# Attention scores by seven half-size products, with key and value forms streamed from HBM by group

## The chip, the cores and the metric

The kernel runs on one core of one Trainium2 chip. The metric is the device time of one execution in microseconds (us), the median of the runs of one session. The trace is that of one execution, taken by the hardware profiler. TensorE (PE) multiplies matrices into PSUM banks, VectorE (DVE) and ScalarE (ACT) work on PSUM and SBUF, GpSimdE (POOL) does small work, and SyncE (SP) issues nearly all DMAs. Each engine takes its instructions in order and waits on semaphores.

## The reference, cut to what matters

A conformer block over `x` of 2 x 4000 tokens of width 512, in bf16:

```
x1 = x + 0.5 * silu(ln(x) @ w_ff1_a) @ w_ff1_b
h = ln(x1); q = h @ w_q; k = h @ w_k; v = h @ w_v
p = softmax(einsum('btd,bsd->bts', q, k) * D**-0.5)
x2 = x1 + einsum('bts,bsd->btd', p, v) @ w_o
x3 = x2 + convolution module (gated, depthwise of 3 taps, batch norm, silu, w_pw2)
out = ln(x3 + 0.5 * silu(ln(x3) @ w_ff2_a) @ w_ff2_b)
```

The change concerns the scores, the product of queries and keys, in the third line.

## The kernel before

The 8000 tokens are cut into 16 chunks of 508 (the last of each sequence, chunks 7 and 15, has 444). The program goes through the first feed-forward chunk by chunk, then attention chunk by chunk, then the rest of the convolution and the second feed-forward. Its order is the order in which the Python code emits instructions, engine by engine; there is no planner. `tick` and `after(n, ...)` put work off by n steps.

Attention is a loop over query chunks `g` and, in each, over 32 key steps `kt` (L1587). One step emits, in this order: the scores of one key tile of 128 keys (`scores`, L1387: four matmuls of 128x508, accumulated over the four slices of the 512 features, into one of three PSUM banks s0, s1, s2 in turn); their exponentials by ACT (`exp_pair`, L1434); what is left of chunk g-1 (`units_late`); value products and Vector sums of chunk g (`units`); the query projection of chunk g+1 (`next_queries`, `q_group`); a hook; and the change of sequence (`keys_swap`). The hook puts the convolution of chunks g-1 and g-2 beside the attention (`pair`: two products `conv_b` and `conv_a`, then the taps L1936 and L1943, and a statistic L1946) and the layer norm of chunk g-1 (statistics L771, aggregate L776, a POOL step L778, L783, and four ACT normalisations).

Value products already use the seven-product scheme (Strassen's, in Winograd's form). A pair of key tiles by 508 queries is a 2x2 block matrix: two tiles by two halves of the queries. `pair_sums` (L1446) forms four block sums on DVE (L1463, bf16) for one or two pairs at a time and adds to the softmax denominators (L1476, f32); `pv` (L1481) multiplies a form of the values by a form of the exponentials, 254 columns wide, seven products over all 15 pairs, each in a bank of its own; `pv_join` (L1514, its adds L1527) puts them together at the end. The products of a chunk's last group and their joins are emitted in the first steps of the next chunk: steps 0 and 1, then two products in steps 2 to 6 (`late_third`), of which the last is read by a join (`pv_join` 5, L1527). In step 2 the denominators are split and sent through DMA transposes; five ticks later they are reduced (L1824) and inverted (L1827). `project` (L1837) multiplies the attention output of chunk g-1 by the folded weights, tile by tile in steps 9 to 12, each followed by a residual on DVE (L923) and a layer norm statistic (L771).

The feed-forward uses the same scheme for its first matmul (`ff_quad`, L1087): products 1 and 5 in one step, 2 and 6 two steps later, 7 and 3 three steps after that, 4 another three steps on, with two Vector additions (L1119) put off by one step.

The forms of the values (V4, V12) lie in SBUF for all 15 pairs. For sequence 0 DVE makes them in chunk 0 (`v_here`); for sequence 1 it makes them ahead in chunks 1 to 5, a pair in ten steps (`v_ahead`, its sums at L1552), stores them in HBM and loads them when the sequence changes.

Of the kernel before, what the change touches and what calls it, by code (L numbers as in the profile page):

```python
# [16 lines left out]
TPC = 4  # L17
# [9 lines left out]
PAIRS = 15  # L27
HC, HD, HF = CHUNK // 2, D // 2, FC // 2
# [231 lines left out]
class Conformer:  # L260
# [31 lines left out]
    def memory(self):  # L292
        nc = self.nc
        self.XR = Region(nc, "xt", (self.SLOTS + 1) * 4096)
# [40 lines left out]
        self.P30, self.b_P30 = self.XR.view(8192 + 10 * 1536, CHUNK), self.XR.buf("P30", 8192 + 10 * 1536, row)  # L335
# [62 lines left out]
        def both(Q, o, m):  # L398
            b = [Q.buf("VF", o + i * m * 2 * HD, m * 2 * HD) for i in range(PAIRS)]
            return b, [Q.view(o + 2 * j * m * 2 * HD, min(2, PAIRS - 2 * j) * m * HD).rearrange("p (n m d) -> p n m d", m=m, d=HD)  # L400
                       for j in range(FC // 2)]

        self.b_V4, self.V4 = both(C, oP, 1)
        self.b_V12, self.V12 = both(self.XR, 8192, 2)
        o = TCB * 4096
        self.hp = [A.view(o + 4 * j * 1024, min(2, PAIRS - 2 * j) * 2 * D).rearrange(
            "p (n k e d) -> p n k e d", k=2, e=2, d=HD) for j in range(FC // 2)]
        self.vhd = nc.dram_tensor("vhd", [PAIRS, 128, 2 * D], BF16, kind="Internal").ap()
        self.v4d = nc.dram_tensor("v4d", [PAIRS, 128, HD], BF16, kind="Internal").ap()
        self.v12d = nc.dram_tensor("v12d", [PAIRS, 128, 2 * HD], BF16, kind="Internal").ap()  # L410
        self.b_vhd = [Buf("vhd") for _ in range(PAIRS)]
        self.b_v4d, self.b_v12d = [[Buf("vfd") for _ in range(PAIRS)] for _ in range(2)]
# [974 lines left out]
    def scores(self, g, kt):  # L1387
        s, W = g % TCB % 2, width(g)
        kc, kj = divmod(kt, TPC)
        ps, b_ps = self.sbank()  # L1390
# [29 lines left out]
    def next_queries(self, g, kt, at):  # L1420

        if g + 1 < NCK and g != 1 and at <= kt < at + TPC:
            self.fetch_queries((g + 1) // TCB, (g + 1) % TCB, kt - at)
        if g == 0 and 24 <= kt < 24 + TPC:
            self.fetch_queries(0, 2, kt - 24)
        if g + 1 < NCK and kt in ((3, 4, 12, 14) if g == 1 else (14, 16, 18, 20)):
            self.q_group((g + 1) // TCB, (g + 1) % TCB, (3, 4, 12, 14).index(kt) if g == 1 else (kt - 14) // 2)

    def p_home(self, g, i):

        n = (16 * g + i) % self.NR
        return n, (16 * g + i) % self.NTS, self.Ft[(8 * g + i // 2) % 2], self.b_F[(8 * g + i // 2) % 2]
# [13 lines left out]
    def pair_sums(self, g, j, step):  # L1446
# [3 lines left out]
        i, n = 2 * j, min(2, PAIRS - 2 * j)  # L1450
        r, m, ft, b_f = self.p_home(g, i)
        R = self.Rt[:, r:r + n, :, 0:hw]
# [4 lines left out]
        s4, s1, s2 = [ft[:, k, 0:n, 0:hw] for k in range(3)]  # L1457
# [12 lines left out]
        sig = [ft[:, 0:2, k, 0:hw] for k in range(n)]  # L1470
        if j == 0:
            if step == 4:
                S.op("DVE", lambda e: e.tensor_tensor(out=acc, in0=sig[0], in1=sig[1], op=ALU.add),
                     reads=b_f[0:2], writes=[self.b_acc[s]])
# [6 lines left out]
    def pv(self, g, n, pairs):  # L1481
# [3 lines left out]
        for i in pairs:  # L1485
            r, m, ft, b_f = self.p_home(g, i)
            R, T, f = self.Rt[:, r], [t[:, m] for t in self.Tt], ft[:, :, i % 2]
            he, ho, v4, v12 = self.h[2 * i], self.h[2 * i + 1], self.V4[i // 2][:, i % 2], self.V12[i // 2][:, i % 2]
            b_he, b_ho, b_v4, b_v12 = self.b_h[2 * i], self.b_h[2 * i + 1], self.b_V4[i], self.b_V12[i]
            form, b_1, mv, b_2 = {1: (he[:, 0:HD], b_he, T[0], self.b_T[0][m]), 2: (ho[:, 0:HD], b_ho, R[:, 0], self.b_R[r]),  # L1490
                                  3: (ho[:, HD:D], b_ho, f[:, 0], b_f[0]), 4: (v4[:, 0], b_v4, R[:, 1], self.b_R2[r]),
# [62 lines left out]
    def v_here(self, j, step):  # L1554
        n = min(2, PAIRS - 2 * j)
        self.v_sums(self.hp[j], self.V4[j][:, :, 0], self.V12[j], self.b_h[4 * j:4 * j + 2 * n], self.b_V4[2 * j:2 * j + n],
                    self.b_V12[2 * j:2 * j + n], step)
# [6 lines left out]
    def v_ahead(self, i, step):  # L1564
# [9 lines left out]
        else:  # L1574
            self.store(self.vhd[i], x, b_x, [self.b_vhd[i]])
            self.store(self.v4d[i], f1, b_1, [self.b_v4d[i]])
            self.store(self.v12d[i], f2, b_2, [self.b_v12d[i]])

    def v_back(self, j, which):
        pairs = range(2 * j, min(2 * j + 2, PAIRS))  # L1580
        src, b_src, dst, b_dst, k = ((self.vhd, self.b_vhd, self.hp[j].rearrange("p n k e d -> p n (k e) d"), self.b_h, 2),
                                     (self.v12d, self.b_v12d, self.V12[j], self.b_V12, 1),
                                     (self.v4d, self.b_v4d, self.V4[j], self.b_V4, 1))[which]
        self.load(dst.rearrange("p n m d -> p n (m d)"), src[pairs[0]:pairs[-1] + 1].rearrange("n p d -> p n d"),
                  b_dst[k * pairs[0]:k * (pairs[-1] + 1)], reads=[b_src[i] for i in pairs])

    def attention(self, old, hook):  # L1587

        for g in range(NCK):
            W = width(g)  # L1590
            for kt in range(KT):
                if kt == self.TAIL_AT:
                    self.tail_scores(g)
                if kt < KT - 1:
                    ps, b_ps = self.scores(g, kt)
# [8 lines left out]
                self.units(g, kt)  # L1604
                self.next_queries(g, kt, 9 if g else 0)
                hook(g, kt)
                self.keys_swap(g, kt)
# [893 lines left out]
```

## Time and profile before

| what | value |
|---|---|
| median of 3 runs (lowest, highest) | 1915.6 us (1914.35, 1915.68) |
| the profiled execution's own time | 1915.51 us |
| its span, first to last instruction | 1911.7 us |
| PE busy in the span | 1896.3 us, 99% |
| DVE busy | 1436.5 us, 75% |
| ACT busy | 1093.2 us, 57% |
| mean DMA rate | 83 GB/s |
| attention, from the page's slices and the timeline | about 410 to 1425 us |
| one ordinary chunk of attention (timeline, from one tail store to the next) | 65.5 us |

Busy times are sums over the span, so a share below 100% tells nothing of one stage. A matmul in the tables has a duration that overlaps its neighbours; its cost is the distance of starts. A group's line gives its count, busy time, mean duration and the idle time of its engine just ahead of it, with what ended that idle time. In the timeline, consecutive instructions of one kind are merged.

### The profile page before, as it was taken

Reading aid. Unit: us, or ns where it says so; the run is one execution under the profiler, and the core shown is the slowest. Engines: PE = TensorE matmul, PEld = TensorE weight load, DVE = VectorE, ACT = ScalarE, POOL = GpSimd, SP = SyncE. Lnnn points to the kernel's source line nnn. Section 1 sums busy time; section 2 is a strip of 40 time slices with the busy share of each in tenths; the row PEclk is TensorE's granted clock in tenths of the full one; section 3 lists DMA queues with packets and bytes.
Section 4 is the critical chain, followed back from the end, with each engine's and each line's share of the span. In section 5 each row is a group of like instructions: output and inputs, shape, how many; then the busy total and the mean of one; then the engine's idle time right before and its main releaser. Section 6 shows DMA issues by size and latency. Waiting matters only on the chain.

```text
span 1911.7 us, 35270 instructions
## 1 busy us (share of the span) xinstructions
PE 1896.3 (99%) x14183; PEld 1401.1 (73%) x14186; DVE 1436.5 (75%) x2991; ACT 1093.2 (57%) x1865; POOL 123.7 (6%) x235
## 2 busy tenths in 40 slices
PE   9999999999999999999999999999999999999998
PEld 6899999966666656666666566666665899999897
DVE  7788888756657667666766676667688888888885
ACT  5677777744443544444434444443447677777774
POOL 1000000000000000000000000000002000000000
PEclk9999999999999999999999999999999999999999
DMA  8233344373222332114821211121146222312211
GB/s 187 72 87 87 79 115 108 88 218 107 77 70 75 96 86 71 54 50 96 197 68 50 55 29 52 52 58 26 51 110 207 62 70 67 76 49 53 64 43 43
DMA packets 286778, 158.03 MB, mean 83 GB/s; under 512 B 204552, under 2 KB 273355, under 8 KB 286351
## 3 DMA queue, kind: packets, MB, share of 16 engines
q1 hardware_dynamic: 285929, 155.37, 31.4%
q8 instruction: 113, 1.85, 0.4%
q14 instruction: 58, 0.48, 0.1%
q10 hardware_dynamic: 678, 0.34, 0.1%
HBM read 62.24 MB, written 48.18 MB: 58 GB/s over the span
## 4 chain that ended last, share of the span: by engine, by line
PE 94%; DVE 4%; ACT 1%; DMA 1%; SPq 0%; issue 0%; POOL 0%; POOLq 0%; DVEq 0%
PE s L658 51%; PE y L658 43%; DVE work L771 1%; DMA keys<-keysd 0%; DVE sums L1463 0%; ACT work L708 0%; DVE xt L923 0%; SPq L716 0%; DVE work L1476 0%; DVE xt L1552 0%; DMA work<-work 0%; DVE work L1824 0%; SPq L712 0%; DVE wff L1946 0%; DVE wff L1943 0%
## 5 line engine op out<-in xcount | busy, mean ns | idle before, releaser
L708 ACT ACTIVATE sums<-s 128x508 bf16<-128x508 f32 (+2 forms) x592 | 347.0, 586 | 456.0 <-PE s L658 453.2
L658 PE MATMUL s<-work,keys 128*128 128x508 bf16 (+3 forms) x2240 | 505.7, 357 | 1.4 <-ACT work L708 1.4
L658 PEld LDWEIGHTS s<-work,keys 128*128 128x128 bf16 (+1 forms) x2240 | 192.0, 97 | 161.7 <-issue 9.5
L708 ACT ACTIVATE keys<-s 128x508 bf16<-128x508 f32 (+1 forms) x281 | 163.8, 586 | 176.4 <-PE s L658 112.4
L658 PE MATMUL y<-work,keys 128*127 128x256 bf16 x1920 | 244.7, 273 | 0.0
L658 PEld LDWEIGHTS y<-work,keys 128*127 128x127 bf16 x1920 | 216.3, 137 | 5.2
L1463 DVE TENSOR_TENSOR sums<-sums 128x508 bf16<-128x508 bf16 (+3 forms) x512 | 190.2, 398 | 27.6 <-ACT sums L708 19.9
L658 PE MATMUL y<-wff,keys 128*127 128x256 bf16 (+3 forms) x1592 | 209.4, 276 | 0.4 <-DVE xt L1010 0.2
L771 DVE BATCH_NORM_STATS2 work<-xt 127x6 f32<-127x512 bf16 x311 | 199.2, 681 | 2.7 <-DMA xt<-in_x_dram 2.6
L658 PE MATMUL y<-sums,keys 128*128 128x254 bf16 (+1 forms) x1440 | 197.8, 269 | 0.0
L658 PE MATMUL s<-sums 128*128 128x254 bf16 x1296 | 194.4, 273 | 0.9 <-DVE s L1119 0.9
L658 PEld LDWEIGHTS y<-sums,keys 128*128 128x128 bf16 x1440 | 139.4, 97 | 66.7 <-issue 0.6
L658 PEld LDWEIGHTS y<-wff,keys 128*127 128x127 bf16 (+1 forms) x1592 | 175.9, 136 | 15.0 <-issue 3.3
L658 PE MATMUL s<-work,wff 128*128 128x508 bf16 (+4 forms) x884 | 185.3, 352 | 0.9 <-ACT work L708 0.6
L708 ACT ACTIVATE work<-xt,work 127x512 bf16<-127x512 bf16 x204 | 164.7, 808 | 14.1 <-DVE work L783 12.7
L969 DVE TENSOR_TENSOR keys<-keys 128x1016 bf16<-128x1016 bf16 x240 | 160.3, 680 | 2.8 <-ACT keys L708 0.7
L778 POOL TENSOR_TENSOR work<-work 127x4 f32<-127x4 f32 (+1 forms) x76 | 77.1, 1014 | 1139.9 <-DVE work L776 1139.9
L658 PE MATMUL s<-work 128*127 128x512 bf16 (+2 forms) x557 | 143.2, 382 | 1.2 <-DVE work L2109 1.2
L658 PE MATMUL y<-sums,xt 128*128 128x254 bf16 (+1 forms) x960 | 141.7, 269 | 0.6 <-DVE sums L1463 0.5
L1476 DVE TENSOR_TENSOR work<-work,sums 128x508 f32<-128x508 f32 (+1 forms) x208 | 139.9, 673 | 2.1
L658 PEld LDWEIGHTS s<-sums 128*128 128x128 bf16 x1296 | 126.6, 98 | 19.3 <-DVE s L1119 1.3
L658 PE MATMUL y<-work,wff 128*128 128x254 bf16 (+1 forms) x892 | 135.3, 274 | 0.0
(155 smaller groups left out, 2350.4 us busy)
## 6 DMA issues: line engine op xcount, KB each, us to landing
xd<-xt SPq DMA_DIRECT2D x28, 448.0 KB, 3.0
xt<-xd SPq DMA_DIRECT2D x28, 448.0 KB, 3.4
out_dram<-xt SPq DMA_DIRECT2D x14, 448.0 KB, 3.2
dcvd<-wff SPq DMA_DIRECT2D x48, 127.0 KB, 2.3
keys<-dcvd SPq DMA_DIRECT2D x12, 508.0 KB, 4.6
xt<-in_x_dram SPq DMA_DIRECT2D x13, 448.0 KB, 4.5
wff<-in_w_ff_b_dram SPq DMA_DIRECT2D x8, 512.0 KB, 7.3
keys<-keysd SPq DMA_DIRECT2D x32, 128.0 KB, 2.8
```

The lines of the kernel that those rows point to most:

```text
L658: self.S.op("PE", lambda e: e.matmul(out, lhsT, rhs, start=start, stop=stop, **kw), reads=reads, writes=[bank], inc=stop if inc is None el ...
L708: return self.S.op("ACT", lambda e: e.activation(out, in_, func, **kw), reads=reads, writes=writes)
L771: self.S.op("DVE", lambda e: e.bn_stats(self.st[sl][:, ti, 0:6], x), reads=[b_x], writes=[self.b_st[sl][ti]])
L778: S.op("POOL", lambda e: e.tensor_tensor(out=self.rs[sl][:, 0:n], in0=self.mv[sl][:, 0:n, 1], in1=self.neghalf[0:TILE, 0:n], op=ALU.pow), ...
L969: self.S.op("DVE", lambda e, out=out, x=x, y=y, op=op: e.tensor_tensor(out=out, in0=x, in1=y, op=op), reads=rd, writes=wr)
L1463: S.op("DVE", lambda e: e.tensor_tensor(out=out, in0=x, in1=y, op=op), reads=rd, writes=wr)
L1476: S.op("DVE", lambda e: e.tensor_tensor(out=acc, in0=acc, in1=sig[step - 4], op=ALU.add), reads=b_f[0:2] + [self.b_acc[s]], writes=[self.b ...
```

## The change

The scores of 28 of the 31 full key tiles are made by seven half-size products, in the 14 chunks that are not the first of a sequence. Four tiles (a quad: key tiles 4q+2 to 4q+5) are taken in four steps. The 2x2 blocks are two pairs of key tiles by two halves of the features, and two halves of the features by two halves of the queries. Key forms are made by DVE in chunks 0 and 8 (`k_sums`), stored in HBM and streamed back, one quad at a time, into two buffers (`k_stream`, 384 KB); query forms are made at the end of the chunk before (`q_sums`). Two of the value forms (V12) are now also stored and streamed by group in every chunk but chunk 0 (`v_stream`). The groups of pairs are shifted by one (the first has one pair, the other seven two). All score work of a quad stays in three banks: c (s0), x (s1), h (s2). Other users of those banks get fixed ones (`ASIDE`).

```diff
+    def score_quad(self, g, q, step):
...
+        def product(k, ps, b_ps, start=False):
+            (a, b_a), (m, b_m) = forms[k]
+            for u in range(2):
+                for j in range(2):
+                    self.mm(ps[:, u * hw:(u + 1) * hw], a(u, j), m(j), start and u == 0 and j == 0, u == 1 and j == 1,
+                            [b_a(u), b_m(j)], b_ps, skip_group_check=True)
...
+        def plus(out, b_out):
+            S.op("DVE", lambda e: e.tensor_tensor(out=out, in0=h[:, 0:W], in1=m5, op=ALU.add),
+                 reads=[b_h, b_m5], writes=[b_out])
+
+        if step == 0:
+            product(1, c, b_c, True)
+            self.act(h[:, 0:W], c[:, 0:W], AF.Copy, [b_c], [b_h])
+            product(5, x, b_x, True)
+            self.act(m5, x[:, 0:W], AF.Copy, [b_x], [b_m5])
+        elif step == 1:
+            product(6, h, b_h)
+            plus(x[:, 0:W], b_x)
+            product(2, c, b_c)
+            exp(c[:, 0:W], b_c, 11)
+        elif step == 2:
+            product(7, h, b_h)
+            plus(m5, b_m5)
+            product(3, x, b_x)
+            exp(x[:, 0:W], b_x, 12)
+            exp(m5, b_m5, 22)
+        else:
+            product(4, h, b_h)
+            exp(h[:, 0:W], b_h, 21)
+
+    ASIDE = {3: (5, 7), 4: (5, 7), 5: (5, 7), 6: (5, 7), 16: (0,), 20: (0,), 21: (1,)}
...
+                if plain and kt < KT - 1 or kt < 2 or kt == KT - 2:
+                    ps, b_ps = self.scores(g, kt, None if plain else self.bank((0, 2)[kt] if kt < 2 else 0))
...
+                elif not plain and kt < KT - 2:
+                    self.score_quad(g, *divmod(kt - 2, 4))
...
+    def forms(self, g, kt):
+        plain, more = g % TCB == 0, g + 1 < NCK and (g + 1) % TCB
+        if more and 27 <= kt < 31:
+            self.q_sums(g + 1, kt - 27)
+        q, r = divmod(kt - 6, 4)
+        if plain:
+            if 0 <= q < QUADS and r < 2:
+                for n in (2 * r, 2 * r + 1):
+                    self.k_sums(g, q, n)
...
+        else:
+            q, r = divmod(kt + 3, 4)
+            if r == 0 and (q < QUADS or more) and q > 1:
+                self.k_stream(g + q // QUADS, q % QUADS)
...
     def units_late(self, o, kt):
-        elif 9 <= kt < 9 + TPC:
-            self.project(o, kt - 9)
+        for ti in {9: (0, 1), 13: (2, 3)}.get(kt, ()):
+            self.project(o, ti)
...
     def units(self, g, kt):
+        j, r = divmod(kt - 3, 4)
+        if 0 < j < GROUPS:
+            if j == 1 and r == 0:
+                for n in (1, 3, 5, 6):
+                    self.pv(g, n, self.group(0))
+            for n in (((1, 3), (5,), (6,), (7,)) if j == 1 else ((1, 3), (7,), (5,), (6,)))[r]:
...
+        j, r = divmod(kt - 1, 4)
+        if 0 < j < GROUPS and r < 3:
+            for n in ((0, 1, 2), (3, 4), (5,))[r]:
                 self.pair_sums(g, j, n)
...
-        here, there = ((22, 27), (3, 8)) if any_score else ((22, 26), (3, 13))
+        here, there = ((22, 27), (3, 8)) if any_score else ((24, 28), (3, 5))
...
             if g and kt == 9 and not any_score:
-                self.ln_job(g - 1, "in", "ACT", (1, 2, 3, 4, 5, 6, 6, 7, 8, 9), slot=0)
+                self.ln_job(g - 1, "in", "ACT", (1, 2, 5, 6, 7, 8, 8, 9, 10, 11), slot=0)
```

The query projections of chunk g+1 move from steps 14, 16, 18 and 20 to steps 16, 17 (two) and 20; the tail's scores go from ahead of step 22 to the end of step 21, with their store and loads on SP; the joins of the last group move together into step 0 (two of them) and step 1. `q_sums` is four DVE subtractions of 128x508 bf16 in steps 27 to 30, `k_sums` four DVE operations of 128x512 bf16 a quad and a store, `v_stream` one load of up to 256 KB a group.

More of the change, by code (lines that the diff above doesn't have):

```diff
@@ L397, in memory @@
         oWvo = take(4096)
[L398 to L407, printed above, removed]
+        self.V4 = C.view(oP, PAIRS * HD).rearrange("p (n d) -> p n d", d=HD)
@@ L1469, in pair_sums @@
             return
-        sig = [ft[:, 0:2, k, 0:hw] for k in range(n)]
+        sig = [ft[:, 0:2, at + k, 0:hw] for k in range(n)]
         if j == 0:
-            if step == 4:
-                S.op("DVE", lambda e: e.tensor_tensor(out=acc, in0=sig[0], in1=sig[1], op=ALU.add),
-                     reads=b_f[0:2], writes=[self.b_acc[s]])
+            S.op("DVE", lambda e: e.tensor_copy(acc, sig[0]), reads=b_f[0:2], writes=[self.b_acc[s]])
         elif step - 4 < n:
@@ L1576, in v_ahead @@
             self.store(self.v4d[i], f1, b_1, [self.b_v4d[i]])
-            self.store(self.v12d[i], f2, b_2, [self.b_v12d[i]])
+            self.store(self.v12d[1][i], f2, b_2, [self.b_v12d[1][i]])
     def v_back(self, j, which):
[L1580 to L1583, printed above, removed]
@@ new lines, in q_sums @@
+    def q_sums(self, g, step):
+        S, s, hw = self.S, g % TCB % 2, width(g) // 2
+        q = lambda e, h: self.qT[s][:, 2 * e:2 * e + 2, h * hw:(h + 1) * hw]
+        t1, t2, t4, t3 = [f[:, :, 0:hw] for f in self.QF]
+        b1, b2, b4, b3 = [[b] for b in self.b_QF]
+        out, x, y, rd, wr = ((t1, q(0, 1), q(0, 0), [], b1), (t2, q(1, 1), t1, b1, b2), (t3, q(1, 1), q(0, 1), [], b3),
+                             (t4, q(1, 0), t2, b2, b4))[step]
+        S.op("DVE", lambda e: e.tensor_tensor(out=out, in0=x, in1=y, op=ALU.subtract), reads=rd + self.b_qT[s], writes=wr)
```

239 lines of the change are left out of this document (152 added, 87 removed).

## The prediction

> **What bounds the kernel now.** I read the page first. Its slices show PE full in all stages and the other engines below it; the chain that ended last is 94% PE.
>
> ```profile
> PE   9999999999999999999999999999999999999998
> DVE  7788888756657667666766676667688888888885
> ...
> PE 94%; DVE 4%; ACT 1%; DMA 1%; SPq 0%; issue 0%; POOL 0%; POOLq 0%; DVEq 0%
> ```
>
> Next come the windows of single stretches: two in attention, each from one tail store to the next, and one in the first feed-forward (columns: PE, PEld, DVE, ACT, POOL busy, granted clock, DMA share, GB/s).
>
> ```profile
> 636.80:702.30 65.50, 65.50 (x431) 40.23 (x430) 47.41 (x101) 29.43 (x50) 3.31 (x9) 1.00 0.30 85
> 1153.75:1219.25 65.50, 65.50 (x432) 40.25 (x431) 44.11 (x87) 29.43 (x50) 3.53 (x9) 1.00 0.19 47
> ...
> 200.00:264.00 64.00, 64.00 (x589) 60.73 (x588) 57.20 (x118) 49.84 (x85) 5.05 (x5) 1.00 0.39 97
> ```
>
> The reader is to see that PE has no gap in attention: a chunk is its PE work, 65.5 us. So PE work removed is time won, and each wait put into PE's queue is time lost in full. DVE has 18 to 21 us to spare in a chunk, ACT 36. Third come the groups kept apart by shape, for prices.
>
> ```profile
> L658 PE MATMUL s<-work,keys 128*128 128x508 bf16 x1736 | 443.6, 377 | 1.4 <-ACT work L708 1.4
> L1463 DVE TENSOR_TENSOR sums<-sums 128x508 bf16<-128x508 bf16 x392 | 153.4, 418 | 25.6 <-ACT sums L708 19.1 <-DVE sums L1463 0.5
> L1476 DVE TENSOR_TENSOR work<-work,sums 128x508 f32<-128x508 f32 x182 | 123.9, 681 | 1.8
> L1119 DVE TENSOR_TENSOR s<-s,sums 128x508 f32<-128x508 f32 x108 | 74.9, 694 | 34.5 <-PE s L658 22.8 <-ACT keys L708 11.7
> ```
>
> Last, the timeline around key steps 6 and 7 of a chunk (start, duration, idle before).
>
> ```profile
> 1185.74 1.02 PE L658 MATMUL s<-work,keys 128*128 128x508 bf16 x4
> 1186.60 1.46 PE L658 MATMUL y<-sums,work 128*128 128x254 bf16 x12
> 1188.53 1.03 PE L658 MATMUL s<-work,keys 128*128 128x508 bf16 x4
> 1188.63 0.69 DVE L1527 TENSOR_TENSOR work<-y,sums 128x508 bf16<-128x508 f32 x1 [2.02 <-PE y L658]
> 1189.83 1.21 DVE L1824 TENSOR_REDUCE work<-work 127x4 f32<-127x1024 bf16 x1
> 1191.17 0.72 DVE L1943 SCALAR_TENSOR_TENSOR wff<-wff,work 128x508 bf16<-128x508 bf16 x1
> 1191.93 0.69 DVE L1946 BATCH_NORM_STATS2 wff<-wff 128x6 f32<-128x508 bf16 x1
> ```
>
> It shows starts, which are costs: four matmuls of 508 columns 0.86 us (1185.74 to 1186.60); twelve of 254 columns 1.30 us (to 1187.90, where the next begin), so four 0.435. It shows too that DVE works on for 4 us from the moment step 6's products end: join, a pair sum, reduce, reciprocal, taps, statistic. Today PE waits for none of that.
>
> **What is removed.** In a changed chunk 28 tiles cost 28 x 0.86 = 24.1 us; 7 quads x 7 products cost 49 x 0.435 = 21.3. PE saves 2.8 us a chunk (2.4 in the two of 444), 12 x 2.8 + 2 x 2.4 = 38 us in all. [...]
>
> **What is added to PE's queue: waits.** A quad in steps a, a+1, a+2, a+3: product 7 opens step a+2 and writes bank h, which DVE's first addition (`plus`) must have read; product 4 opens step a+3 and needs the second `plus`; product 6 opens step a+1 and needs ACT's copy. Behind a waiting product stand all later products of the chunk, and behind them all stages. DVE takes its queue in order, so `plus` waits for all that was emitted before it. The compiled order of a changed chunk, priced by starts, gives the following: `plus` 0.69, pair sum 0.36 (0.43 when it needs the last), denominator add 0.62, join 0.61, reduce and reciprocal 1.34, tap 0.75, statistics 0.60, residual L923 0.67; DVE and ACT begin 0.20 after a product's last issue (1199.35 + 0.86, then DVE at 1200.41), and PE some 0.05 after them (estimate; ACT to DVE is 0.03 at 1209.14).
>
> A. Step 6 ends with products that `pv_join` 5 reads. DVE then has join 0.1 + 0.61, pair sum 0.36, denominator 0.62, reduce and reciprocal 1.34, tap and statistic 1.36, and only then `plus` 0.69 and 0.05: 5.1 us. PE meanwhile has products 6 and 2 and 16 value matmuls: 2.6. Product 7 in step 8 waits 2.5 us.
> B. Behind this `plus`: denominator 0.62, tap 0.69, second `plus` 0.69; PE has one step of 1.3. Product 4 waits 0.6.
> C. Two projections in step 9. From the first one's end: second residual starts at 1.06, +0.67, three pair sums 1.2, statistic 0.60, pair sum 0.36, denominator 0.62, statistic 0.60, `plus` 0.69, 0.05: 5.85 us; PE has 0.86 + 0.44 + 1.5 + 1.75 = 4.55. Product 7 in step 12 waits 1.3.
> D. The same in steps 13 to 16 with two matmuls less on PE: 1.5.
> E. ACT in steps 16 to 19 has two query copies and layer norms of 0.81 us ahead of the copy c to h: walking its queue, products 5 and 6 wait 0.4 and 0.3: 0.7.
> F. In step 26 the ACT part of a tap (0.71) follows both copies, DVE's part follows that, and `plus` of step 27 follows it: from the step's start 1.07 + 0.05 + 0.59 + 0.60 (copies, tap on ACT) + 0.75 + 0.69 = 3.8 against 3.06 of PE: 0.7.
> G. Key forms of quad 6: the load is issued behind the tail's store and four loads, 3.7 us after step 22 begins (the store came 0.46 after the tail's products, the loads ended at +3.7 by the timeline at 1219.25). It lands after 3.0 (256 KB rows) to 5.2 (512 KB rows), at 6.7 to 8.9; needed at 7.4. 0 to 1.5; middle 4.1: 0.4. The other loads have 9 us and more.
> H. Three small ones (product 4 in step 13, 5 in step 22, a value product in step 31): 0.1 each.
>
> Sum 8.0 us of waits in an ordinary chunk, minus 2.8: +5.2. Eleven such (2 to 6, 9 to 14): +57. Chunk 7, 444 wide: 7.1 - 2.4 = +4.7. Chunk 1 has no taps yet (A 1.2, B, E, F none): 4.7 - 2.8 = +1.9. Chunk 15 has no next queries: 5.9 - 2.4 = +3.5. `v_ahead` puts two sums of 0.29 into one of these chains in each of chunks 1 to 5: +2.5. `k_sums` costs DVE 28 x 0.42 (row L1552 of 128x512) in chunks 0 and 8, beside PE that waits there only for pair sums: 0 to 4, I take 1, near nothing, as chunk 8 leaves DVE more than 10 us; if that cover fails in chunk 0, 4. `q_sums` run where nothing of PE waits for DVE (steps 30, 31, 0, 1 use plain scores or none). Elsewhere the order stays: 0.
>
> Sum: 57 + 4.7 + 1.9 + 3.5 + 2.5 + 1 = 71 us. The profiled execution took 1915.51 (span 1911.7 and 3.8 around it), the median is 1915.6: **1986 us**.
>
> **Rivals.**
> 1. The waits are hidden and it is faster: 1915.5 - 38 + 1 = 1879. For it: the feed-forward runs the same seven products with DVE at 57.2 of 64.0 us, 89%, and PE lost 2.2 us in 108 quads (releases by L1119). Attention would have 44.1 to 47.4 + 11 of 62.7, 88 to 93%. The mechanism is distance: there three steps lie between `plus` and its reader. It decides when the chains A, C and D are shorter than PE's work beside them, all waits of a chunk together below 2.8 us. Against: A without any `plus` is 3.9 us of shown DVE starts against 2.6 of PE. Chance 0.13, spread over 1875 to 1911.
> 2. Only A stalls, the rest is absorbed as PE comes later: 2.5 - 2.8 a chunk: 1913, within a few us. Against: C and D start from PE's own products, so a late PE does not help. 0.07.
> 3. Transfers are late too: 68 MB more of loads (384 KB x 98, 1.9 MB of V12 x 15) behind 31% of DMA time; G at 1.5 and one more such wait: 14 x 2.5 = 35 more, 2021. For it: chunk 7 to 8 has a DMA share of 0.73 already. 0.10.
> 4. The clock falls in A's wait. Row: between 1906 and 1910 us PE is idle (last products end near 1905.5) and the granted clock is 0.80, so an idle stretch of some 3 us is enough. A's 2.5 us is close; each fall costs about 0.8 us by that row, 14 of them 11 us: 1997. [...] 0.05.
> The remaining 0.65 is my forecast, 1940 to 2015. That the scores are not halved as said is excluded by the order: 196 products of 254 columns a chunk are there.
>
> **The range** is 1930 to 2020: A, C and D alone (5.3 - 2.8 a chunk) give about 1950, with each 0.5 shorter 1930; rival 3 gives the upper end. Runs of this kernel tell apart about 0.2%, 4 us. Faster: rival 1 and a part of 2, 0.16; same: 0.04; slower: 0.80.
>
> **What would show it.** PE waits in `s` products released by DVE's `plus`, about 5 a chunk, the longest near 2.5 us at step 8; an ordinary chunk of 70.7 instead of 65.5 us; PE busy near 89% in attention; DVE about 55 to 58 us a chunk; waits on DMA of the key forms below 0.5 a chunk. I am wrong if a chunk takes less than 65 us, if the waits at steps 8, 12 and 16 are absent, or if they are released by ACT or DMA.

## The result, and the profile after

The changed kernel takes 2069.1 us (median; 2066.2 to 2075.0) beside 1915.3 us before: a ratio of 1.081, 95% interval 1.078 to 1.083. The forecast was 1986 us, its range 1930 to 2020: the sign was right, and more than half of the loss was not foreseen. The profiled execution took 2068.2 us, with a span of 2064.2.

The page of the changed kernel answers to the first fence of the prediction.

```profile
PE   9999999988988888998898899889888999999998
DVE  6888888667668777776777777777787888888885
...
PE 70%; DVE 16%; DMA 6%; issue 3%; ACT 3%; SPq 2%; POOL 0%; DVEq 0%; POOLq 0%; ACTq 0%
```

PE is no longer full in attention (slices 8 to 30, counted from 0), and the chain that ended last, 94% PE before, now goes through Vector for 16% and through DMAs for 6%. The windows of two chunks, each from one tail store to the next, say how much (columns as before):

```profile
1268.02:1340.76 72.74, 65.55 (x520) 47.59 (x519) 54.99 (x108) 36.81 (x65) 2.47 (x9) 1.00 0.42 108
1340.76:1415.26 74.50, 65.82 (x514) 47.77 (x513) 54.19 (x107) 36.41 (x64) 2.47 (x9) 0.98 0.42 105
```

These two chunks take 72.7 and 74.5 us (the others, by their tail stores, 67.3 to 78.0), where an ordinary one took 65.5 and the prediction had 70.7. In the second one the granted clock is 0.98: something the prediction gave a chance of 0.05. The view of the waits names what PE waited for (total us, times, longest):

```profile
PE s L666 <- DVE s L1680: 68.4, 52, 3.6
PE s L666 <- DMA xt<-kfd: 31.1, 14, 5.3
PE y L666 <- DVE keys L1565: 11.8, 4, 7.7
PE s L666 <- DVE sums L1477: 7.3, 12, 1.2
PE s L666 <- ACT work L716: 5.3, 13, 1.4
```

L1680 is `plus`, `kfd` are the key forms in HBM, L1565 makes value forms in chunk 0, L1477 are pair sums. To compare kernels I added up over each whole trace by how much every matmul starts later than full clock allows after the one before it (0.108 us for 254 columns, 0.215 for 508, by the starts from 1185.74 on in the prediction's timeline), and put each delay to what released the matmul (such a delay is some 0.16 us longer than the idle time that the timeline prints, as a matmul's duration overlaps the next one). Before the change this comes to 24 us, after it to 213. The rise of 189 less the rise of the time, 152.7, leaves 36 us: the saving, forecast at 38. With that 36, the sum gives the profiled time of every kernel below within 1 us (added matmuls counted where there are any), so nothing but PE's delays is left to explain. This is an account of where PE's time went; the causes are tested by the experiments.

Step 8, where the prediction had its largest wait (A), looks like this:

```profile
1305.06 0.69 DVE L1540 TENSOR_TENSOR work<-y,sums 128x508 bf16<-128x508 f32 x1 [1.00 <-PE y L666]
...
1306.72 1.22 DVE L1957 TENSOR_REDUCE work<-work 127x4 f32<-127x1024 bf16 x1
...
1308.07 0.72 DVE L2076 SCALAR_TENSOR_TENSOR wff<-wff,work 128x508 bf16<-128x508 bf16 x1
1308.82 0.69 DVE L2079 BATCH_NORM_STATS2 wff<-wff 128x6 f32<-128x508 bf16 x1
1309.42 0.68 DVE L1680 TENSOR_TENSOR s<-s,xt 128x508 f32<-128x508 f32 x1
...
1310.16 0.61 PE L666 MATMUL s<-xt,keys 128*128 128x254 bf16 x4 [2.42 <-DVE s L1680]
```

Vector runs without a pause from the join at 1305.06, and `plus` begins at 1309.42, though product 6, which it adds, was issued by 1305.41. PE stands 2.42 us.

### The profile page after: what moved, and what is told of

Its sections match the earlier page's. It is cut to its first block, busy times and chain, and to the rows that moved or that the text cites. A ratio compares the mean times of both kernels' runs of the same rounds, so it can differ in the third digit from the quotient of the medians.

```text
span 2064.2 us, 38821 instructions
## 1 busy us (share of the span) xinstructions
PE 1915.1 (93%) x15362; PEld 1510.9 (73%) x15362; DVE 1601.7 (78%) x3315; ACT 1190.4 (58%) x2061; POOL 110.7 (5%) x235
## 3 DMA queue, kind: packets, MB, share of 16 engines
q8 instruction: 123, 2.02, 0.4%
## 4 chain that ended last, share of the span: by engine, by line
PE 70%; DVE 16%; DMA 6%; issue 3%; ACT 3%; SPq 2%; POOL 0%; DVEq 0%; POOLq 0%; ACTq 0%
PE y L666 37%; PE s L666 33%; DVE sums L1477 3%; DVE work L779 2%; DMA xt<-kfd 2%; DMA pqd<-wff 2%; DVE s L1680 2%; DVE xt L931 1%; SPq L1904 1%; ACT work L716 1%; DVE work L1957 1%; DVE work L1488 1%; DVE wff L2076 1%; DVE work L1540 1%; ACT wff L716 1%
## 5 line engine op out<-in xcount | busy, mean ns | idle before, releaser
L716 ACT ACTIVATE sums<-s 128x508 bf16<-128x508 f32 (+2 forms) x494 | 289.0, 586 | 359.7 <-PE s L666 357.2
L666 PE MATMUL s<-work,keys 128*128 128x254 bf16 (+5 forms) x1456 | 229.3, 294 | 3.2 <-ACT work L716 1.4
L1477 DVE TENSOR_TENSOR sums<-sums 128x508 bf16<-128x508 bf16 (+3 forms) x512 | 191.3, 398 | 33.3 <-ACT sums L716 27.9
L666 PE MATMUL y<-sums,keys 128*128 128x254 bf16 (+1 forms) x1440 | 203.1, 272 | 11.8 <-DVE keys L1565 11.8
L666 PE MATMUL s<-xt,keys 128*128 128x254 bf16 (+1 forms) x816 | 129.6, 277 | 73.1 <-DVE s L1680 68.4
L666 PE MATMUL y<-work,wff 128*128 128x254 bf16 (+2 forms) x1116 | 184.0, 292 | 0.0
L666 PEld LDWEIGHTS s<-work,keys 128*128 128x128 bf16 (+1 forms) x1456 | 116.9, 98 | 58.7 <-ACT work L716 8.4
L666 PEld LDWEIGHTS s<-xt,keys 128*128 128x128 bf16 x816 | 74.0, 99 | 117.1 <-DVE s L1680 83.1
L666 PE MATMUL s<-xt 128*128 128x254 bf16 (+1 forms) x784 | 120.7, 277 | 40.2 <-DMA xt<-kfd 31.1
L1488 DVE TENSOR_TENSOR work<-work,sums 128x508 f32<-128x508 f32 (+1 forms) x224 | 151.1, 675 | 3.9
```

What stands on the lines that cost most here:

```text
L666: self.S.op("PE", lambda e: e.matmul(out, lhsT, rhs, start=start, stop=stop, **kw), reads=reads, writes=[bank], inc=stop if inc is None el ...
L716: return self.S.op("ACT", lambda e: e.activation(out, in_, func, **kw), reads=reads, writes=writes)
L1477: S.op("DVE", lambda e: e.tensor_tensor(out=out, in0=x, in1=y, op=op), reads=rd, writes=wr)
L1488: S.op("DVE", lambda e: e.tensor_tensor(out=acc, in0=acc, in1=sig[step - 4], op=ALU.add), reads=b_f[0:2] + [self.b_acc[s]], writes=[self.b ...
```

## The experiments

The numbers of all kernels, for reference. "Plus", "key forms" and "value forms" are delays of PE by what released them; windows at half clock are of 3.413 us, those behind the last matmul left out. Delays and windows are those of the profiled execution, whose time lies up to 5 us from the median. The kernel before was between 1916.4 and 1916.9 us in these sessions.

| kernel | median us | ratio, 95% interval | all delays us | plus | key forms | value forms | windows at half clock |
|---|---|---|---|---|---|---|---|
| after the change | 2069.1 | 1.081 (1.078 to 1.083) | 212.6 | 86.5 | 33.4 | 1.4 | 18 |
| e1 keys early | 2048.2 | 1.068 (1.066 to 1.070) | 197.1 | 95.0 | 0 | 7.4 | 18 |
| e2 join late | 2044.3 | 1.067 (1.065 to 1.069) | 188.3 | 55.6 | 40.2 | 1.9 | 11 |
| e3 statistics late | 2071.9 | 1.082 (1.080 to 1.084) | 212.8 | 52.3 | 56.3 | 0.9 | 26 |
| e4 key stores by ACT | 2078.3 | 1.084 (1.082 to 1.085) | 224.9 | 85.0 | 41.2 | 2.9 | 23 |
| e5 quad 6 first | 2050.1 | 1.070 (1.068 to 1.071) | 189.3 | 95.7 | 1.9 | 8.9 | 12 |
| e6 all stores by ACT | 2066.1 | 1.077 (1.075 to 1.079) | 212.7 | 82.8 | 41.3 | 1.7 | 21 |
| e7 reordered | 2013.4 | 1.049 (1.047 to 1.051) | 160.4 | 30.4 | 8.3 | 29.5 | 11 |
| e8 fillers | 2071.8 | 1.081 (1.078 to 1.083) | 196.7 | 68.8 | 40.7 | 4.1 | 14 |
| e9 tail later | 2077.9 | 1.083 (1.081 to 1.086) | 220.4 | 25.3 | 0 | 0 | 27 |
| e10 combined | 2005.6 | 1.046 (1.043 to 1.048) | 153.9 | 29.9 | 26.6 | 3.1 | 13 |
| e11 streams by ACT | 2044.4 | 1.067 (1.065 to 1.068) | 186.8 | 96.3 | 0 | 0 | 13 |
| e12 combined, streams by ACT | 1976.0 | 1.031 (1.029 to 1.033) | 121.3 | 33.0 | 0 | 0 | 5 |

**Vector's order: e2 and e3.** The theory is that `plus` is late because of what is emitted ahead of it on Vector. e2 undoes this at step 8:

```diff
-            self.pv_join(o, 6 if n == 2 else 5)
+            if n == 2 or o == NCK - 1:
+                self.pv_join(o, 6 if n == 2 else 5)
...
+        elif kt == 7:
+            self.pv_join(o, 5)
-                self.sums_by_query(o % TCB % 2, 5)
+                self.sums_by_query(o % TCB % 2, 7)
```

> Join 5 is emitted in step 7 right behind the first plus, the reduce and reciprocal at the end of step 8 instead of step 6; nothing else changes. Vector-order theory: the wait of product 7 in step 8 (2.5 us in 13 chunks, 33 us in all) goes to under 0.5; what is moved makes the chain ahead of step 12 longer by 0.5 to 1.2 us (10 us in all); the 8 half-clock windows behind step 8's waits go, but one or two come behind step 12: 2069 - 33 + 10 - 10 = 2036, between 2024 and 2048. Rival, turnaround: the wait is the distance PE to DVE to PE by itself and not what stands ahead of plus; the wait in step 8 stays above 2 us and the time within 5 us of 2069.

It took 2044.3 us, 25 less. In the timeline of its PE product 7 of step 8 (at 1290.40) waits no more; the second `plus` costs 0.54 us (0.36 before), the waits of steps 12 and 16 stand where they stood, and a new one of 0.57 comes from a residual, which now waits for the later reciprocal.

```profile
1290.40 0.60 PE L666 MATMUL s<-xt,keys 128*128 128x254 bf16 x4
1292.41 0.61 PE L666 MATMUL s<-xt,keys 128*128 128x254 bf16 x4 [0.54 <-DVE xt L1680]
1295.76 0.61 PE L666 MATMUL s<-work,keys 128*128 128x254 bf16 x4 [0.57 <-DVE xt L931]
1300.38 0.61 PE L666 MATMUL s<-xt,keys 128*128 128x254 bf16 x4 [0.88 <-DVE s L1680]
1309.00 0.61 PE L666 MATMUL s<-xt,keys 128*128 128x254 bf16 x4 [1.10 <-DVE s L1680]
```

Turnaround alone is thereby excluded: the wait was the queue. e3 does the same for steps 12 and 16:

```diff
-                self.ln_job(g - 1, "in", "ACT", (1, 2, 5, 6, 7, 8, 8, 9, 10, 11), slot=0)
+                self.ln_job(g - 1, "in", "ACT", (4, 4, 8, 8, 9, 10, 10, 11, 11, 12), slot=0)
```

> The layer norm statistics of chunk g-1 are emitted behind the second plus (end of steps 12 and 16 instead of 9, 10, 13 and 14), its aggregate and normalisations two steps later; nothing else changes. Vector-order theory: 1.2 us of Vector work leaves the chains of steps 9 to 11 and 13 to 15, so the waits at steps 12 (1.04) and 16 (1.26 us) go to 0 to 0.2 in 13 chunks: 27 us less; ScalarE's queue waits at steps 16 to 19 move to 18 to 21, plus or minus 4; few half-clock windows hang on these waits: 2042, between 2033 and 2052. Rival: these waits start at the projection's end and are set by residuals and pair sums alone; under 10 us less.

Delays behind `plus` fell by 34 us, more than expected, and the time did not move: 2071.9. The trace says where the gain went. The transposes of the normalised rows are now on SP right ahead of the tail:

```profile
1262.60 3.81 SPq L724 DMA_TRANSPOSE work<-work  x3
1266.45 1.05 SPq L605 DMA_DIRECT2D xd<-xt  x2
1267.55 0.88 SPq L733 DMA_DIRECT2D pqd<-wff  x1
1270.27 1.74 SPq L1904 DMA_DIRECT2D wff<-pqd  x4
1272.05 0.43 SPq L720 DMA_DIRECT2D xt<-kfd  x1
```

PE reaches quad 6 sooner, its load is issued as late as ever, and the wait on key forms grew from 33.4 to 56.3 us, with eight more windows at half clock behind it. What one queue gave, the next one took.

**The key forms: e1, e5, e11.** e1 issues all their loads one step earlier, e5 only that of quad 6, at the front of step 21, and e11 leaves the steps and sends all streamed loads through ScalarE's queue.

```diff
# e1
-            q, r = divmod(kt + 3, 4)
+            q, r = divmod(kt + 4, 4)
# e5
                 if kt == 21:
+                    if not plain:
+                        self.k_stream(g, 6)
                     self.tail_scores(g)
# e11, in k_stream and v_stream
-        self.load(..., reads=...)
+        self.load(..., eng="ACT", reads=...)
```

> The loads of the key forms are issued one step earlier (the load for quad 6 in step 20 instead of 21, ahead of the tail's store and its four loads on SP); nothing else changes. Queue theory: product 5 of quad 6 waits 33 us in all (14 waits of 0.8 to 5.5) because its load stands behind the tail's DMAs in SP's order; these waits fall below 3 us in all, and the half-clock windows that follow them in the changed kernel (7 of 3.41 us, some 12 us of time) go with them: 2069 - 42 = 2027, between 2018 and 2036. Rival, bandwidth: the streams themselves are too slow (112 GB/s mean, 42% of DMA time); an earlier issue only moves the wait: over 20 us of waits on the key forms stay and the time is above 2050.

> Only the load of the key forms of quad 6 is put first in step 21, ahead of the tail's store and its loads; all others stay where the change puts them. Queue theory, mended by what the earlier issue of all loads showed (SP then waits for the buffer itself, with all behind it): product 5 of quad 6 waits under 5 us in all instead of 33, no wait on the value forms or on the Vector sums of chunks 1 and 2 is added, and the half-clock windows behind the long ones (7 of 18) go: 2069 - 29 - 9 = 2031, between 2022 and 2042. Rival, bandwidth: the load takes so long beside the value forms that over 15 us of its waits stay, above 2050.

> The changed kernel with every load of the key and value forms issued from ScalarE's queue instead of SP's, in the same steps; nothing else changes. Queue theory: the 33 us of waits on quad 6's key forms come from SP's order (transposes, the tail's store and loads, row loads ahead of it), so they fall below 5 us, with the half-clock windows behind them; the issues take ScalarE 14 x 0.35 us a chunk, which adds some 4 us to waits on it: 2069 - 29 - 9 + 4 = 2035, between 2020 and 2050. Rival, landing: all DMAs share the same 16 engines, and a load issued in time still lands late beside transposes and the other streams: over 15 us of waits on key forms stay, above 2050.

They took 2048.2, 2050.1 and 2044.4 us. In all three the wait on key forms is gone (0, 1.9 and 0 us), so the queue was the cause and not bandwidth: e11 moves the same bytes in the same steps. In the changed kernel SP shows it plainly; the load of quad 6 is the fifth entry:

```profile
1265.67 1.19 SPq L724 DMA_TRANSPOSE work<-work  x1
1266.91 1.05 SPq L605 DMA_DIRECT2D xd<-xt  x2
1268.02 1.02 SPq L733 DMA_DIRECT2D pqd<-wff  x1
1270.89 1.75 SPq L1904 DMA_DIRECT2D wff<-pqd  x4
1272.67 0.43 SPq L720 DMA_DIRECT2D xt<-kfd  x1
```

The load's issue is 4.65 us behind the tail's store; 2.9 us of it pass before the first of the four loads, which wait for that store's landing. In the kernel before, 1.5 us passed there, and the four loads were done 3.3 us behind the store:

```profile
1219.25 0.34 SPq L725 DMA_DIRECT2D pqd<-wff  x1
1220.76 1.75 SPq L1771 DMA_DIRECT2D wff<-pqd  x4
```

But the three kernels gained 21, 19 and 9 us less than I expected, and the reason I gave after e1, that SP stood at a buffer not yet free, is refuted by e5 and e11, which show the same. What grew is `plus`, by 9 to 10 us, half of it in chunk 2, where a delay of 2.2 us became one of 6.6. In e11 Vector idles there for the rows from which it makes the value forms ahead, the next late item of the same pile on SP:

```profile
606.34 0.69 DVE L1488 TENSOR_TENSOR work<-work,sums 128x508 f32<-128x508 f32 x1
612.51 0.62 DVE L1565 TENSOR_TENSOR wff<-wff 128x256 bf16<-128x256 bf16 x2 [5.49 <-DMA wff<-keysd]
```

In the changed kernel the same load came as late, and PE lost the time at the key forms first. The wait on key forms is 33 us in the changed kernel and 40 to 41 in e2, e4, e6 and e8, which do not touch quad 6: there the load lands 3.8 to 3.9 us after its issue on average instead of 3.5, and PE comes to it 0.1 to 0.3 us sooner. Why it lands later stays open.

**Chunk 0: e4 and e6.** e4 takes the stores of the key forms off SP, e6 those of the value forms too.

```diff
# e4, k_sums (e6: v_here likewise)
-            self.store(self.kfd[b][q], ...)
+            S.dma("ACT" if g == 0 else "SP", ..., lambda e: e.dma_start(self.kfd[b][q], ...), ...)
```

> In chunk 0 alone the stores of the key forms are issued from ScalarE's queue instead of SP's; nothing else changes. Queue theory: the store of quad 0 stands behind twelve key loads on SP, k_sums of quad 2 waits for it 10 us on Vector, and value sums behind k_sums hold PE; with another queue the waits of chunk 0 (12 us) and its three half-clock windows (5 us) go: 2069 - 16 = 2053, between 2048 and 2058. Rival, work: Vector has too much to do in chunk 0 (28 key sums of 0.42 us beside the value sums), and a store in time only moves the wait: under 6 us less, above 2062.

> In chunk 0 the stores of key forms and of value forms are all issued from ScalarE's queue; nothing else changes. Queue theory: Vector's wait of 10 us at 435 to 445 us and PE's of 12 us behind it come from stores standing behind key loads in SP's order; they go, with the three half-clock windows: 2069 - 16 = 2053, between 2047 and 2060. Rival, bandwidth: the DMA engines are 99% busy from 425 to 445 us (6.6 MB with the key loads and a 1 MB weight load), a store lands late from any queue, and the wait moves again: above 2062.

e4 took 2078.3 us, e6 2066.1. In the changed kernel Vector stands at a key sum, whose buffer waits for the store of quad 0. That store was issued at 437.46, behind a run of twelve key loads, a weight load of 1 MB and three more key loads, and landed 8.1 us later:

```profile
445.54 0.43 DVE L1642 TENSOR_TENSOR xt<-keys 128x512 bf16<-128x512 bf16 x1 [10.17 <-DMA kfd<-xt]
```

In e4 it stands as long one step on, for the other store:

```profile
447.55 0.43 DVE L1565 TENSOR_TENSOR xt<-keys 128x512 bf16<-128x512 bf16 x1 [9.46 <-DMA v12d<-xt]
```

In e6 neither is there: Vector's longest wait before 462 us is 1.54, and PE's delays behind the value forms' sums fall from 12.4 to 3.7 us. So the queue theory holds for the wait in chunk 0 as well, although the DMA engines were busy for 0.83 of the time from 425 to 445 us in the changed kernel (0.99 only from 440 to 445); that the store of the changed kernel also landed slowly (8.1 us, against 4.8 in e6, where it is issued at 424.04) is a share that no run parts from the late issue. By their totals both runs lie where their rivals had them, above 2062: in e4 the wait moved to the other store, and e6 fell by 3 us only. There the wait on key forms came out 8 us longer, and three more windows ran at half clock. A single repair worth 9 us cannot be read from the total here; it has to be read from the row.

**The clock: e8, d1, d2.** In the changed kernel 18 windows of 3.413 us run at half clock. PE is busy for 53.2 of their 61.4 us, and its matmuls start at twice the usual distance there (from 646.93 to 650.24: 0.21 us for 254 columns, 0.427 for 512, beside 0.108 and 0.216), so half of that, some 27 us, is lost; a window in which PE is busy throughout costs 1.7. They all begin on one grid of 3.413 us (at 445.44, where three follow each other, 534.19, 646.83 and so on, each a whole number of 3.413 us behind the first). Two equal waits at step 8, of 2.41 us by the timeline, show what decides (windows of the changed kernel cut on that grid; the second column is PE busy, the seventh the clock):

```profile
643.41:646.83 3.42, 1.01 (x10) 0.75 (x9) 3.35 (x7) 0.72 (x1) 0.00 (x0) 1.00 0.85 245
646.83:650.24 3.41, 3.41 (x15) 2.06 (x13) 2.30 (x4) 1.81 (x3) 0.00 (x0) 0.50 1.16 257
718.51:721.92 3.41, 1.79 (x17) 1.35 (x14) 3.31 (x6) 1.15 (x2) 0.00 (x0) 1.00 0.34 119
721.92:725.33 3.41, 2.26 (x18) 1.76 (x19) 3.38 (x7) 1.52 (x4) 0.00 (x0) 1.00 0.90 182
```

The first wait lies in one window, PE is busy for 1.01 of 3.41 us, and the next window runs at half clock although PE is full in it. The second wait is cut by a border, and nothing happens. d1 and d2 put waits of known length into the kernel before the change:

```diff
+                if g and kt in (17, 24) and not self.any_score:
+                    for k in range(4 + g):      # d1: 14 + 2 * (2 * g - 2 + (kt == 24))
+                        self.S.op("POOL", lambda e: e.memset(self.dose, 0.0), reads=[] if k else [b_ps], writes=[self.b_dose])
+                    self.gate = [self.b_dose]   # read by the next step's scores
```

> The kernel before the change, with two artificial waits of PE in each of chunks 1 to 15 (steps 18 and 25): PE's scores wait for a chain of 14, 16, ... 72 small GpSimd fills released by the step before, which are no part of the computation. It measures what a wait costs. Grid theory (from the changed kernel, where all 15 falls fit): the clock is set for fixed windows of 3.413 us, and a window runs at half clock if PE stood idle for 2.0 us or more of the window before it; waits under 2.0 us cost only themselves, waits of 2.0 to 4 us are followed by a fall or not as they lie in the grid (about 40% of those of 2.0, all of those over 4), each fall 1.7 us. Rival, single waits: every wait above some length between 2.0 and 2.6 is followed by a fall, wherever it lies. Rival, activity: falls come from the mean load of a chunk, and here, at 95% busy, there are fewer than three. Time: 1916 + 90 of waits + 18 falls x 1.7 = 2036, between 1980 and 2080.

> As the dose before, with chains of 5 to 19 fills instead of 14 to 72, the same in both places of a chunk, so that PE's waits run from about 1.4 to 3.7 us (the earlier doses gave 0.167 us a fill). Grid theory: no fall behind a wait under 2.0, some 40% of those of 2.2, some 85% of those of 3.7, each decided by whether a window of the 3.413 us grid holds 2.05 to 2.15 us or more of idle time; some 13 falls in all; 1916 + 76 + 13 x 1.7 = 2014, between 1995 and 2035. Rival, single waits: one length parts all waits with falls from all without.

Each was run once. d1 took 2209.6 us: a fill took 0.167 us and not the 0.1 I had assumed, so its waits ran from 2.9 to 12.8 us, and 70 windows fell. d2 took 2010.4, with 11 windows. In d2 a delay of 2.17 us at 706 was followed by a fall and one of 3.52 us at 1272 was not:

```profile
703.73:707.14 3.41, 1.40 (x10) 0.67 (x8) 3.31 (x6) 1.67 (x3) 0.89 (x8) 1.00 0.63 181
707.14:710.55 3.41, 3.41 (x12) 1.52 (x11) 0.03 (x1) 1.19 (x2) 0.00 (x0) 0.50 0.75 235
1266.93:1270.34 3.41, 1.93 (x11) 0.88 (x9) 3.34 (x7) 2.82 (x5) 0.62 (x6) 1.00 0.26 52
1270.34:1273.75 3.41, 1.53 (x10) 0.93 (x11) 1.43 (x3) 0.48 (x1) 1.16 (x11) 1.00 0.68 169
1273.75:1277.17 3.42, 3.42 (x22) 2.01 (x21) 1.08 (x3) 1.31 (x4) 0.00 (x0) 1.00 0.24 85
```

So no length of a single wait parts the two, and the rival of single waits falls; the sum of idle time in a window does. The rival of the mean load falls too: it had fewer than three falls at 95% busy, which is d2's load (1916 of 2010 us), and d2 had 11 windows. Over all 16 traces, every full-clock window with 2.16 us or more of delay in it was followed by one at half clock, none with less than 2.02 was, and between the two both occur. Where the program starts in the grid differs from trace to trace: the first border of a window lies 1.71 us after the first instruction in the changed kernel and 0.58 us in d2 (from the half-clock windows at 646.83 and 707.14).

e8 tests it the other way round: 14 matmuls more in the wait of step 8.

```diff
+            if q == 1 and g > 1:
+                for k in range(14):
+                    self.mm(c[:, 0:hw], part(0, 0)[0](0, 0), q_at(0, 0)[0](0), True, True, [...], b_c, inc=k == 13)
             product(7, h, b_h)
```

> The changed kernel with work added: 14 matmuls of 254 columns, no part of the computation, into bank c ahead of product 7 in step 8 of each chunk from 2 on (1.5 us, inside the wait of 2.5 us that stands there). Grid theory: PE's idle time there falls to 1.1 us, below the 2.05 to 2.15 at which windows fell in all traces so far; the 8 falls behind step 8's waits go, nothing is lost as the wait covers the matmuls: 2069 - 8 x 1.7 = 2055, between 2048 and 2062, faster with more work. Rival: the clock answers to single waits of any kind or to the load of a chunk, falls stay as they were, and the matmuls cost nothing or their own 1.5 us: 2069 to 2091.

```profile
1308.62 1.68 PE L666 MATMUL s<-work,keys 128*128 128x254 bf16 x14
1311.19 0.61 PE L666 MATMUL s<-xt,keys 128*128 128x254 bf16 x4 [0.89 <-DVE s L1680]
```

Product 7 waits 0.89 us behind the fillers, and of the eight falls behind step 8 only that of chunk 15 is left, where the wait is the longest; the others follow waits on DMA, in chunk 0 by way of Vector. That falls go with a shorter wait fits both theories; what parts them is d2. But other waits ate the gain: key forms 7 us more, value forms 3. The time is 2071.8, unchanged with some 20 us of added PE work. The mechanism is shown, the gain of 14 us is not.

**Together: e7, e9, e10, e12.** e7 joins e5, e6, the first part of e2, and e3 with more of Vector's work behind the second `plus` (the second denominator adds, two taps, the query forms). e9 moves the tail to step 25 and the normalisations to one a step; e10 takes what had held; e12 is e10 with the streams through ScalarE's queue.

```diff
# e7, e9, e10, e12: the second denominator add one step later
-            for n in ((0, 1, 2), (3, 4), (5,))[r]:
+            for n in ((0, 1, 2), (3, 4), (5,) if j == GROUPS - 1 or g % TCB == 0 else (), () if g % TCB == 0 else (5,))[r]:
# e9, e10, e12: the tail
-                if kt == 21:
+                if kt == (21 if plain or self.any_score else 25):
# e10, e12: rests of taps
-        self.after(1, rest)
+        self.after({0: 2, 3: 8}.get(cc, 1), rest)
```

> All together, the same instructions in another order: quad 6's load first in step 21, chunk 0's stores from ScalarE, join 5 behind plus in step 7, the second denominator add of each group behind the second plus, statistics behind the second plus of steps 12 and 16, two taps and the query forms moved behind the second plus too. Vector-order theory: A, C, D and F (2.5, 1.0, 1.3, 0.7) go to under 0.2 each, B to 0.1, E stays at 0.7, G under 0.4, chunk 0 below 3 us, and nearly all half-clock windows go, since no single wait is over 2 us: 1915.5 - 38 + 14 x 1.8 + 4 = 1907, between 1895 and 1940. Rival, Vector is simply full in attention (58 of 63 us of PE work): whatever the order, waits come back elsewhere; over 80 us of waits stay and the time is above 1970.

> The reordered kernel with the tail's scores, store and four loads in step 25 instead of 21 (quad 6's load back in its place), and the normalisations one to a step in steps 18 to 21. Queue theory: what was left of waits on streams in the reordered kernel (29 us on value forms, 8 on key forms) came from SP, where transposes, tail and row loads now stand together in steps 20 to 22; these waits fall below 10 us in all, and ScalarE's 11 to 6: 2013 - 34 - half of the 19 us of slow clock = 1970, between 1950 and 1990. Rival, the DMA engines or Vector are full: over 25 us of waits on streams stay, or come back as waits on Vector; above 1998.

> What held so far together: chunk 0's stores from ScalarE, join 5 behind plus, the second denominator adds and two rests of taps behind the second plus, statistics behind the second plus of steps 12 and 16 with the normalisations where the reordered kernel had them (steps 18 to 20, so that the convolution does not wait for them as it did with the tail later), the tail's scores and DMAs in step 25. Sum of the removed work and the waits that I expect: C and D 0.6 each, E 0.8, F and step 27 to 31 0.8, others 0.5, so 3.3 a chunk; 1915.5 - 38 + 14 x 3.3 + 10 for chunks 0 and 8 + 5 of slow clock = 1939, between 1920 and 1965: still slower than before the change. Rival, Vector is full: whatever leaves one chain comes back in another, over 80 us of waits more than before the change stay and the time is above 1970.

> The combined kernel with the loads of the key and value forms issued from ScalarE's queue. Queue theory: its 27 us of waits on key forms, 3 on value forms and part of the 10 on layer norm transposes go, with half of its 20 us of slow clock: 2005.5 - 30 - 10 - 3 + 4 = 1967, between 1948 and 1988. Rival, landing or a full ScalarE: the waits stay on the loads or move to ScalarE's copies; above 1992.

They took 2013.4, 2077.9, 2005.6 and 1976.0 us; only the last is near what I expected, and by their totals e7 and e10 lie where the rival of a full Vector had them, above 1970. In e7 `plus` cost 30 us instead of 86, but value forms 29.5, by the same pile on SP. In e9 the streams cost nothing, and the convolution waited 56.6 us for the last transposes of the normalised rows: one normalisation a step is too late for step 24. In e10 the load of quad 6 was issued 3.8 to 4.5 us before PE came to it, right behind three transposes and two stores of 448 KB on SP, and landed only 5.7 to 7.1 us later (26.6 us of waits). With the streams in another queue, e12 has no wait on them:

```profile
PE s L666 <- DVE s L1681: 21.7, 34, 2.1
PE s L666 <- DMA work<-work: 13.1, 6, 2.9
PE s L666 <- DVE sums L1477: 9.8, 15, 2.4
PE s L666 <- ACT work L716: 6.7, 16, 1.4
```

Against the rival of a full Vector speaks that in e12 Vector does the same 3315 instructions as in the changed kernel with 53 us less of waits behind `plus`. For it speaks that what is left, some 5 us a chunk, is spread over many small waits, and I found no place for them, so this rival stays open. Its ordinary chunks take 67 to 71 us against 65.5 before. **No version here beats the kernel before the change.**

## Why the prediction was right in sign and short in size

By its own terms, over the whole kernel, as delays of PE in the profiled execution:

- **Saving: 38 us, measured 36.** Half-size products do cost half, 0.108 us a matmul from start to start beside 0.215 (in the changed kernel the medians are 0.109 and 0.216); the row of the trace held.
- **Vector's chains (A to D, F), about 90 us, measured 86.5.** In the chunk around 1310 us: A 2.5 against 2.58, B 0.6 against 0.52, C 1.3 against 1.05, D 1.5 against 1.26, F 0.7 against 0.66. Walking Vector's queue in emitted order, with durations of the old trace, gave each of them to 0.3 us.
- **E, ScalarE's queue: 0.7 a chunk, measured 0.72.** Right.
- **G, key forms of quad 6: 0.4 a chunk, 6 us in all; measured 33.** The failed step is the time of issue, "3.7 us after step 22 begins", with the need at 7.4: it leaves the load 3.7 us. In the changed kernel PE came to the load between 2.4 us after its issue and 2.2 us before it, on average 1.2 after. The 3.7 was read from the kernel before, where the four loads ended 3.3 us behind the tail's store. After the change the load of quad 6 was issued 4.5 to 6.1 us behind that store, as the four loads waited longer for it (2.9 us instead of 1.5 in the rows shown) and the store itself, behind transposes and other stores on SP, came 0.6 to 4.5 us after the tail's last product (0.6 in an ordinary chunk before). The landing was not the term that failed: it took 3.1 to 3.9 us in thirteen of the fourteen chunks and 4.9 in one, where the sum had 4.1. The longest wait, 5.5 us, is in the chunk with the latest store and the latest issue. The pile on SP and the place of the wait were foreseen; the rival that had more of it (3) put it down to the transfers, was given 0.10 and had 1.5 a chunk, which is also too little.
- **`k_sums` in chunks 0 and 8: 1 us, measured about 12 in chunk 0 alone, and three windows at half clock besides (2.6 us, counted with the clock below).** The failed step priced Vector's work and not the store between two quads, which stood behind the key loads on SP. A new DMA was put into a queue, and I did not walk that queue.
- **The clock: nothing in the forecast, measured some 27 us.** The failed step is that A's wait of 2.5 us was taken as most likely too short to lower the clock: rival 4 had a chance of 0.05, with 14 falls of 0.8 us. There are 18 windows, 8 of them behind A's waits, at 1.5 us each on average. The row the rival rested on, at the end of the program, gave half the price: from 1908.4 on the granted clock is 0.50 there, so the stretch from 1906 to 1910, at 0.80, holds less than half of such a window. Nor could it show that the place of a wait in the grid decides.
- **H, small ones: 0.3 a chunk, 4 us; measured some 10**, of which the value product in step 31 alone waits 0.77 instead of 0.1 in that chunk.

These four terms (27 + 28 + 11 + 6) are 72 of the 82 us between 1986 and the profiled 2068; the rest is in small ones. So the mechanism foreseen, waits behind `plus`, was right in place and size, and alone it gives the sign; the two large terms that were missed lie in the issuing queue and in the clock. Of what the prediction said would show it right, the five waits behind `plus` a chunk, the longest at step 8, PE's 89% (90 and 88 in the two chunks) and nearly Vector's 55 to 58 us (55.0 and 54.2) are there; the chunk of 70.7 us, and waits on key forms under 0.5, are not.

## What to carry to other kernels

When products are split so that a second engine's result stands between two of them, price each of these places by what the second engine's queue holds ahead of it, and emit that work behind the step that PE waits for: this alone was worth 25 us here at one place of a chunk. When loads and stores are added, walk the issuing queue as carefully as an engine's, the stores that free a buffer too: here the pile on SP moved from one waiting load to the next (key forms 33.4 to 56.3 us in e3, value forms 1.4 to 29.5 in e7), and with the queue split, in e11 and e12, no wait on these loads was left. And count the half-clock windows: here one followed each full-clock window of 3.413 us with 2.16 us or more of PE's delays in it, and it cost up to 1.7 us.

## What was not expected of the hardware

In these 16 traces the granted clock changes on a fixed grid of 3.413 us. In the changed kernel every stretch at half clock, the one behind the last matmul left out, is one, two or three times 3.413 us long (646.83 to 650.24, 534.19 to 541.01, 445.44 to 455.68). Behind a full-clock window with 2.16 us or more of delay in it, some 60% of its length, the whole next one ran at half clock, whether PE was busy in it throughout (3.41 of 3.41 us from 646.83) or not (2.73 from 1530.88); behind one with less than 2.02 none did. The grid's place against the start of the program differs from trace to trace. The length of a single wait does not decide: a delay of 2.17 us was enough in d2, and one of 3.52 us, cut by a border, was not. So the same wait, as it happened to lie, was followed by a fall or not (2.41 us at step 8, ending at 646.00 and at 722.71), and a fall cost up to 1.7 us more. The number of falls changed with the edits: between 5 and 27 in the kernels e1 to e12, which but for e8's added matmuls do the same work.
